# Windowed-attention scores in eight 64x32 tiles of 160 keys each, and a new instruction order

## Chip, core and metric

The kernel is one program on one core of a Trainium2 chip. The metric is device time in microseconds (us), from the first to the last instruction of a run, as the median of several runs. One execution was also profiled; all rows below come from that one.

## The reference, cut to what matters

Eight batches, eight heads, 576 positions, head width 64. The first half is causal attention with a window of 128 keys and a linear bias; its output `x` feeds four experts, each a full causal attention of width 64, mixed by the two best gates.

```python
# first half, per batch and head (window = 128)
scores = scale * np.matmul(q, k.transpose(0, 1, 3, 2))
mask = (rel >= 0) & (rel < window)              # rel = query position - key position
scores = np.where(mask, scores + bias[None], -1000000000.0)
attn = softmax(scores); attn_out = np.matmul(attn, v)
# second half, per expert e, x is (8, 576, 512)
q, k, v = x @ wq[e], x @ wk[e], x @ wv[e]
a = softmax(causal(scale * (q @ k.transpose(0, 2, 1))))
ye = a @ v @ wo[e]                               # added to out with the gate's weight where e is chosen
```

## The kernel before

**Work.** The first half goes by groups: one group is one batch and two heads, 32 groups in all. A group's queries stand in four blocks of 128 and a tail of 64. For block `i` the window reaches over the block's own 128 keys and the 128 before them, so `scores` (line 717) multiplies 128 queries by 256 keys (128 for block 0), once for each of the two heads. The operands are `e` (groups 0 to 3) or `r` (groups 4 to 31): one head lies in partitions 0 to 63, the other in 64 to 127, so each product is a 64x128 tile of TensorE (64 rows, 128 columns of weights), and the two heads use its two halves. The tail is one 128x128 product from `r` and `q`. The score blocks land in PSUM banks. `wrap` copies with a mask, so that of the 256 columns the 128 that row `r` needs stand in one place: row `r` of a block needs keys `r+1` to `r+128` of the 256. VectorE then adds the bias and takes the extremum (`softmax_block`), ScalarE does the exponential (`exp_block`), `normalise` multiplies by the reciprocal sum (`scl`: on GpSimd or ScalarE). TensorE transposes the result (`idt,p`), ScalarE, VectorE and GpSimd bring it to SBUF (`pa`), TensorE multiplies it by the values (`pa,vt`, two 128x64 tiles) and `xh` and its remainder `xl` are kept.

**The second half** projects `x` (`qkproj`, `vproj`: `WH`, `WL` with `xh`), forms the experts' scores (`moe_s`: `KSm,QSm`, 64x128 tiles; the tail `KSm,QBm`), normalises, transposes through DRAM (`d`, `mpt`) or on TensorE, multiplies by the values (`mpt,v`, 128x64 tiles) and by `wo` (`moe_wo`). Float32 products are recorded as two matmuls each; those in `float32r` as one.

**Order.** All engine work is first recorded as a list. Then `plan` builds a graph of it, gives each node a rank, and `schedule` walks through time with cost figures of its own, picks the node of highest rank on each engine, the PSUM bank of each result, and the engine of those operations that have alternatives (`nc.any`: a copy from PSUM on ScalarE or VectorE, a rescaling on GpSimd or ScalarE). On TensorE it groups the nodes by the shape of the tile (`_kind`) with a price for a change of it (`_enter`). Where TensorE has nothing to do early on, it adds a filling product on zeros (`fill`, `bank<-QBm` with 256 columns). The numbers in `K` steer all of this. All instructions leave through line 1465 (1478 in the changed file), so groups are told apart by tile names.

Of the kernel before, what the change touches and what calls it, by code (L numbers as in the profile page):

```python
# [34 lines left out]
K = {'dr': 385, 'S': 2, 'T': 2, 'A': 2, 'X': 1, 'M': 1, 'apv': 0, 'alag': 2, 'pvlag': 2, 'vorder': 0, 'na': 0, 'pp': 2, 'tp': 4, 'mp': 3, 'ta0': 0.08, 'ta1': 0.91, 'sa0': 0.1, 'sa1': 1.0, 'sb0': 0.68, 'sb1': 0.77, 'tb0': -0.03, 'tb1': 1.08, 'wo0': 0.1, 'wo1': 0.45, 'wa0': 0.05, 'wa1': 1.3, 'aa0': 0.0, 'aa1': 1.04, 'ab0': -0.04, 'ab1': 1.0, 'xp': 6, 'ts': 1, 'lead': 0, 'pa': 2, 'na0': 2, 'wb0': 0.18, 'wb1': 1.0, 'sh': 0, 'man': 1, 'mode': 'rank', 'wv': 1, 'off': {'AHTmsb': -51319, 'AHTmsc': 226585, 'AHTmsd': 57984, 'AHmsb': 962863, 'AHmsc': -1174046, 'AHmsd': 176548, 'ALTmvb': -352873, 'ALTmvc': 681549, 'ALTmvd': -720993, 'ALmvb': -58580, 'ALmvc': -343133, 'ALmvd': 387548, 'Ggb': -294268, 'Ggc': 358200, 'Ggd': 796547, 'Gvb': 50164, 'Gvc': 356650, 'Gvd': -900704, 'KSmsb': -134466, 'KSmsc': 71203, 'KSmsd': -949465, 'KSmvb': 878611, 'KSmvc': 564812, 'KSmvd': 177012, 'MPLgb': -196142, 'MPLgc': -640724, 'MPLgd': 354521, 'MPLsb': -745879, 'MPLsc': -467463, 'MPLsd': 612374, 'MPLvb': -896678, 'MPLvc': 231527, 'MPLvd': -176829, 'QBmgb': -157372, 'QBmgc': 543347, 'QBmgd': 601313, 'QBmvb': 23180, 'QSmsb': -53771, 'QSmsc': 238376, 'QSmsd': -140325, 'QSmvb': -403396, 'QSmvc': -572336, 'QSmvd': -1126436, 'Qvb': -1083103, 'Qvc': 419856, 'Qvd': 85696, 'WHga0': 215851, 'WHga1': -1349520, 'WHga2': -20302, 'WHga3': -216938, 'WLva0': -987256, 'WLva1': 222553, 'WLva2': -36747, 'WLva3': -289734, 'WOHgb': -356530, 'WOLvb': -286267, 'Wvb': 1153321, 'Wvc': -170954, 'Wvd': -272595, 'bdtgb': -10523, 'cntvb': -146833, 'cntvc': 20870, 'cntvd': 237025, 'dsb': 1203, 'dsc': -165933, 'dsd': 31497, 'dvsb': -495176, 'dvsc': 457438, 'esb': 163420, 'exgb': -68299, 'exgc': 22524, 'exgd': 302310, 'exsb': 101341, 'exsc': -235122, 'exsd': 567186, 'idtsb': 590241, 'lgvb': -151767, 'lgvc': 386501, 'lgvd': 265472, 'maltb': -8751, 'maltc': 334704, 'maltd': -97900, 'matb': -365698, 'matc': 248620, 'matd': -22341, 'mktsb': -419636, 'mpgb': -406012, 'mpgc': 613629, 'mpgd': -154987, 'mpsb': 945412, 'mpsc': 4558, 'mpsd': -362700, 'mptsb': -182897, 'mptsc': 801091, 'mptsd': 314174, 'mpvb': -134103, 'mpvc': 336130, 'mpvd': -599159, 'mrvb': -1116242, 'mrvc': -99062, 'mrvd': -1036577, 'msltb': -129432, 'msltc': -366459, 'msltd': 175381, 'msmvb': 369133, 'mstb': 1203485, 'mstc': 692927, 'mstd': 840517, 'mttd': -325265, 'mttsb': 168397, 'mxvb': -299213, 'mxvc': -478280, 'mxvd': 99527, 'otc': -605153, 'otd': -1396659, 'otsc': 150370, 'otsd': 92453, 'outsc': -133228, 'outsd': -181459, 'paga0': -503470, 'paga1': 249445, 'paga2': -267635, 'paga3': -222708, 'pagb': 181139, 'pagc': 147868, 'pasa0': -38196, 'pasa1': 37112, 'pasa2': -870775, 'pasa3': 155051, 'pasb': 555862, 'pasc': 26055, 'pava0': -620338, 'pava1': -187059, 'pava2': 773026, 'pava3': -655362, 'pavb': 704014, 'pavc': 122636, 'pga0': -2221003, 'pga1': -795897, 'pga2': -130731, 'pga3': -1738506, 'pgb': -53777, 'pgc': 76239, 'psa0': 28304, 'psa1': -185091, 'psa2': 204361, 'psa3': 128899, 'psb': -1536389, 'psc': -386534, 'pva0': 339625, 'pva1': -498595, 'pva2': 68261, 'pva3': 728830, 'pvb': -369118, 'pvc': -142760, 'qktb': -187519, 'qktc': -911093, 'qktd': -1759864, 'qsb': -417280, 'qsc': 71999, 'rsb': -258694, 'rsc': -219196, 'rva0': 51622, 'rva1': 381144, 'rva2': 332157, 'rva3': -218686, 'rvb': -1056049, 'rvc': 484891, 'smvb': 135492, 'sta0': 180586, 'sta1': 91875, 'sta2': 76259, 'sta3': 764898, 'stb': 1475626, 'stc': 351117, 'sva0': 248048, 'sva1': -621166, 'sva2': -209110, 'sva3': -150684, 'svb': -266514, 'svc': -1900487, 'tbtsb': -338384, 'tmsb': 211161, 'tmsc': 447992, 'tmsd': 570421, 'tmtsb': -328856, 'tta0': 166591, 'tta1': -745498, 'tta2': 206031, 'tta3': 487372, 'ttb': -169960, 'ttc': 1223111, 'vgd': 77695, 'vsb': 348165, 'vsc': 629445, 'vsd': 510506, 'vsgb': -166647, 'vsgc': 98885, 'vssb': -74263, 'vssc': 694024, 'vsvb': 85697, 'vsvc': 252966, 'vtb': 316160, 'vtc': 54818, 'vtd': 81004, 'vtsb': -411318, 'vtsc': -108070, 'vvd': -29753, 'wgb': -488048, 'wgc': 850675, 'wgd': -21990, 'wstsb': -513062, 'wsvb': 221204, 'wsvc': -637005, 'wsvd': -102434, 'xhsa0': 522390, 'xhsa1': -221939, 'xhsa2': -523460, 'xhsa3': 183211, 'xhsb': 570069, 'xhsc': 1038764, 'xhva0': 61127, 'xhva1': -6055, 'xhva2': 279616, 'xhva3': 568354, 'xhvb': 161674, 'xhvc': -251466, 'xta0': -614582, 'xta1': 56907, 'xta2': 434532, 'xta3': 445032, 'xtb': 217229, 'xtc': 297371, 'xtta0': -177787, 'xtta1': 546283, 'xtta2': 235747, 'xtta3': 245812}, 'cw': 12, 'lm': 15, 'f0': 900, 'f1': 69640, 'f2': 8574.9424, 'setup': 1254186.7966, 'wt': 0.7926, 'bv': -1660.3072, 'ba': -24824.2265, 'bp': -44128.4556, 'chn': 150, 'l0': 0.5, 'l1': 0.75, 'w0': 0.04, 'w1': 0.83, 'w2': 0.15, 'w3': 1.15, 'hs': 9.253065176954073e+41, 'bz': [21712, 2035, 1615], 'vl': 1, 'wd': 0, 'dx': 300, 'se': 0, 'gl': 1, 'rb': 3, 'early': 4, 'vb': 3, 'la': 4, 'fx': 1, 'fm': 1, 'pt': 7, 'q': 8888, 'ex': 0, 'rq': 0, 'o0': 1, 'dh': 1.6, 'eq': 1, 'wb': 1, 'tbf': 2, 'db': 4, 'es': 0, 'aft': 0, 'nl': 1, 'px': [7], 'ps': 1, 'pn': (), 'af': 210, 'an': 0.84, 'vs': 2, 'tc': 1.04, 'rl': 1.4, 'ku': 3, 'nat': 0, 'at': 32, 'ae': 32, 'xw': 1, 'sv': 1, 'as': 1, 'hold': 0.0, 'gw': 2.9095}  # L35
# [29 lines left out]
def _cost(e, m, a, k):  # L65
# [3 lines left out]
    if e == "tensor":  # L69
        if m == "transpose":  # L70
            return 108.5
        full = a[1].ap[0][1] == P
        wide = _free(a[1]) == P
        if a[1].dtype == F32R:
            return max(n * 0.4475 + 3, 109) if full else max(n * 0.4475 + 4, 110) / 2
        if not wide:
            return n / 1.2 + 3
        return (2 if full else 1) * (max(n / 1.2, 107) + 3)
# [18 lines left out]
def _kind(e, m, a):  # L97
    if e != "tensor":
        return 0
    if m == "transpose":  # L100
        return 1
    if a[1].ap[0][1] != P:
        return 2
    return 3 if _free(a[1]) != P else 1


def _enter(e, m, a):
    if e != "tensor":
        return 0
    return (ENTER, 200, 150)[_kind(e, m, a) - 1] if m != "transpose" else 155  # L110
# [97 lines left out]
def graph(ops, alt):  # L208
# [112 lines left out]
def schedule(g, rank, succ, setup=0.0, wt=0.5, bias=((0, 0, 0, 0, 0),) * 2, fill=(900, 60000, 9999), cw=6, hs=0):  # L321
# [46 lines left out]
    while done < n:  # L368
        while ev and ev[0][0] <= now:
            i = heapq.heappop(ev)[1]  # L370
            q = alts[i]
            if len(q) > 1:
# [9 lines left out]
                eng[i], cost[i], lock[i] = best[1], best[2], port[i][best[3]]  # L382
# [6 lines left out]
        for e in range(5):  # L389
            if not ready[e] or t[e] > now:  # L390
                continue
            if e == 0:
# [9 lines left out]
                sums = [0.0] * 4  # L402
# [99 lines left out]
def plan(ops, alt):  # L502
# [8 lines left out]
    for x in order:  # L511
# [39 lines left out]
def attn_moe_kernel(ctx, tc, hd, rd, vd, wall, wo, mk, tb, tm, mt, ident, out):  # L551
# [163 lines left out]
    def scores(g, u, s, n0):  # L715
# [4 lines left out]
        for i in (2 * u, 2 * u + 1):  # L720
# [324 lines left out]
    def moe_s(b, pr, blocks):  # L1045
# [507 lines left out]
```

## Time and profile before

| | us |
|---|---|
| median of three runs (lowest to highest) | 495.44 (494.18 to 495.81) |
| span of the profiled execution | 493.3 |
| TensorE matmuls busy | 480.1 |
| weight loads busy | 408.1 |
| VectorE busy | 366.6 |
| ScalarE busy | 331.1 |
| GpSimd busy | 259.5 |

The profiled execution's own time is its span, 493.3 us, from its first to its last instruction; the median of the runs is 2.1 us above it. Busy times of different engines overlap. A matmul's record reaches from its start to a modelled end behind the pipeline, so records of one engine overlap too: what a matmul costs is read from the distance of the starts.

### The profile page before, as it was taken

Reading aid. Unit: us, or ns where it says so; the run is one execution under the profiler, and the core shown is the slowest. Engines: PE = TensorE matmul, PEld = TensorE weight load, DVE = VectorE, ACT = ScalarE, POOL = GpSimd, SP = SyncE. Lnnn points to the kernel's source line nnn. Section 1 sums busy time; section 2 is a strip of 40 time slices with the busy share of each in tenths; the row PEclk is TensorE's granted clock in tenths of the full one; section 3 lists DMA queues with packets and bytes.
Section 4 is the critical chain, followed back from the end, with each engine's and each line's share of the span. In section 5 each row is a group of like instructions: output and inputs, shape, how many; then the busy total and the mean of one; then the engine's idle time right before and its main releaser. Section 6 shows DMA issues by size and latency. Waiting matters only on the chain.

```text
span 493.3 us, 13248 instructions
## 1 busy us (share of the span) xinstructions
PE 480.1 (97%) x4259; PEld 408.1 (83%) x4259; DVE 366.6 (74%) x1818; ACT 331.1 (67%) x1240; POOL 259.5 (53%) x572
## 2 busy tenths in 40 slices
PE   7889999999999999999999999999999999999995
PEld 6768988998797989888888888879879878898864
DVE  4577788889979798885959788797687868736510
ACT  3796578778758577773947758496685746536862
POOL 0796574657837529382573728375164836412340
PEclk9999999999999999999999999999999999999999
DMA  7868352575587976596938856688717463567023
GB/s 218 266 181 251 115 147 60 197 251 188 179 284 227 332 247 222 183 295 241 305 127 257 296 201 186 217 280 267 257 69 241 184 236 126 192 225 231 1 86 106
DMA packets 50853, 100.79 MB, mean 204 GB/s; under 512 B 4960, under 2 KB 28640, under 8 KB 50784
## 3 DMA queue, kind: packets, MB, share of 16 engines
q1 hardware_dynamic: 50704, 99.81, 61.8%
q8 instruction: 34, 0.56, 0.5%
q14 instruction: 35, 0.29, 0.2%
q10 hardware_dynamic: 80, 0.13, 0.1%
HBM read 62.05 MB, written 37.88 MB: 203 GB/s over the span
## 4 chain that ended last, share of the span: by engine, by line
PE 72%; DMA 10%; DVE 7%; ACT 6%; POOL 3%; SPq 1%; issue 1%; POOLq 0%; ACTq 0%; DVEq 0%
PE bank L1465 72%; DMA out<-ot 4%; DMA d<-W 2%; DMA e<-in_hd 2%; ACT p L1465 2%; ACT mp L1465 2%; DVE mp L1465 1%; DVE W L1465 1%; POOL p L1465 1%; DMA wst<-in_wall 1%; DVE p L1465 1%; ACT ot L1465 1%; SPq L1465 1%; DVE bank L1465 1%; DVE xh L1465 1%
## 5 line engine op out<-in xcount | busy, mean ns | idle before, releaser
L1465 ACT ACTIVATE p<-p,nm 128x128 f32<-128x128 f32 x288 | 113.1, 396 | 46.9 <-DVE nm L1465 44.9
L1465 POOL TENSOR_SCALAR p<-p,r 128x128 f32<-128x128 f32 x279 | 98.3, 374 | 50.8 <-ACT p L1465 16.5
L1465 POOL TENSOR_SCALAR mp<-mp,mr,w 128x384 f32<-128x384 f32 (+3 forms) x128 | 75.8, 608 | 50.3 <-DVE nm L1465 23.8
L1465 PE MATMUL bank<-xh,WH 128*128 128x288 f32 x512 | 90.0, 302 | 0.0
L1465 PEld LDWEIGHTS bank<-xh,WH 128*128 128x128 f32 x512 | 75.1, 189 | 2.3 <-issue 1.4
L1465 ACT ACTIVATE mp<-mp,mnm 128x512 f32<-128x512 f32 (+3 forms) x128 | 70.2, 551 | 9.5 <-DVE mnm L1465 9.4
L1465 DVE CUSTOM_DVE_ANT_0 p<-bank,tbt 128x128 f32<-128x128 f32 x288 | 70.2, 280 | 0.7
L1465 PE MATMUL bank<-pa,vt 128*64 128x256 f32 (+2 forms) x768 | 59.6, 311 | 1.9 <-DVE pa L1465 1.6
L1465 DVE STREAM_TRANSPOSE W<-mp 128x128 f32<-128x128 f32 (+1 forms) x112 | 53.7, 494 | 8.3 <-DMA d<-W 5.1
L1465 PEld LDWEIGHTS bank<-pa,vt 128*64 128x64 f32 x768 | 43.3, 137 | 18.6 <-DVE pa L1465 2.5
L1465 PE MATMUL bank<-WH,xh 128*128 128x260 f32 x288 | 58.2, 293 | 0.3 <-ACT ot L1465 0.3
L1465 DVE COPY_PREDICATED bank<-mkt,bank 128x256 f32<-128x256 int32 (+2 forms) x160 | 47.7, 325 | 11.7 <-PE bank L1465 11.5
L1465 DVE CUSTOM_DVE_ANT_0 mp<-bank,mtt 128x512 f32<-128x512 f32 (+3 forms) x128 | 54.7, 485 | 1.2 <-PE bank L1465 1.1
L1465 ACT ACTIVATION_READ_ACCUMULATOR p<-p,nm 128x1 f32 x288 | 55.1, 191 | 0.0
L1465 POOL TENSOR_SCALAR_AFFINE_SELECT pa<-pa 128x512 f32<-128x512 f32 x64 | 39.7, 635 | 23.8 <-ACT pa L1465 22.1
L1465 PE MATMUL bank<-xh,WL 128*128 128x288 f32 x256 | 51.7, 297 | 0.0
L1465 PE MATMUL bank<-mpt,v 128*64 128x64 f32 (+4 forms) x576 | 49.3, 319 | 0.2
L1465 PE MATMUL bank<-r 64*128 64x256 f32 (+1 forms) x448 | 49.1, 358 | 0.0
L1465 PE MATMUL bank<-idt,p 128*128 128x128 f32 x288 | 47.2, 277 | 1.6 <-POOL p L1465 1.5
L1465 PEld LDWEIGHTS bank<-WH,xh 128*128 128x128 f32 x288 | 44.8, 189 | 2.2 <-DVE mnm L1465 0.9
L1465 PEld LDWEIGHTS bank<-mpt,v 128*64 128x64 f32 x576 | 27.4, 137 | 21.4 <-issue 15.3
L1465 PEld LDWEIGHTS bank<-r 64*128 64x128 f32 x448 | 37.0, 187 | 5.9 <-issue 2.0
(98 smaller groups left out, 918.7 us busy)
## 6 DMA issues: line engine op xcount, KB each, us to landing
d<-W SPq DMA_DIRECT2D x28, 832.0 KB, 4.7
mpt<-d SPq DMA_DIRECT2D x28, 832.0 KB, 5.4
vt<-in_vd SPq DMA_DIRECT2D x32, 320.0 KB, 3.8
out<-ot SPq DMA_DIRECT2D x32, 256.0 KB, 2.9
r<-in_rd SPq DMA_DIRECT2D x28, 288.0 KB, 4.0
r<-in_hd SPq DMA_DIRECT2D x56, 128.0 KB, 3.9
dv<-vs SPq DMA_DIRECT2D x35, 128.0 KB, 2.8
v<-dv SPq DMA_DIRECT2D x7, 640.0 KB, 4.6
```

The costliest lines, as they stand in the source:

```text
L1465: getattr(getattr(tc.nc, e), m)(*a, **k)
```

## The change

Each 128-query block is cut in four quarters of 32 queries. Quarter `x` (its first query) needs only keys `x+1` to `x+159` of the 256, so it gets its own product of 32 queries by 160 keys (block 0: all 128 keys), written to its own 32 PSUM partitions. With two heads that makes eight products of 64x32 tiles where there were two of 64x128. The rest of the 256 columns is not written any more, so each PSUM bank is written once at the beginning with zeros (`blank`, eight products of 512 columns). `moe_s` gets the same loop, but `K["ms"]` is 1, so it does what it did. `_kind` gives 64x32 tiles a kind of their own.

`K` has new values: besides the ranks by category that were there (`off`), a number for each node (`nd`) that is added to its rank, and for some nodes the alternative to use (`nf`). So the order of every engine is another, and so is the engine of a number of operations.

```diff
-K = {'dr': 385, 'S': 2, 'T': 2, 'A': 2,
...
+K = {'nd': {0: 2095482, 1: 230515, 2: 147409, 3: 778716,
...
+'qs': 4, 'ms': 1, 'dr': 385, 'S': 2, 'T': 2, 'A': 2,
...
 def _kind
     if a[1].ap[0][1] != P:
-        return 2
+        return 4 if _free(a[1]) != P else 2
...
 def schedule
-                eng[i], cost[i], lock[i] = best[1], best[2], port[i][best[3]]
+                x = K["nf"].get(i, best[3])
+                eng[i], cost[i], lock[i] = *q[x], port[i][x]
...
 def schedule_k
+    rank = [r + K["nd"].get(i, 0) for i, r in enumerate(rank)]
...
 def plan
+        if i == alt["blank"][0]:
+            out += [_place(alt["blank"][1], lambda v: alt["banks"][k]) for k in range(BANKS)]
...
 def warm
+        nc.alt["blank"] = (first["QB"], ("tensor", "matmul", (z, QB[:, 0, 0, :], QB.rearrange("p a b n -> p (a b n)")), dict(start=True, stop=True)))
...
 def scores
-            for h in range(2):
-                d = r[D * h : D * h + D]
-                nc.tensor.matmul(ss[h][:, o : o + n], d[:, P * (i + h) : P * (i + h + 1)], d[:, k0 : k0 + n], start=True, stop=True)
+            w = P // K["qs"]
+            for x in range(0, P, w):
+                for h in range(2):
+                    d = r[D * h : D * h + D]
+                    q0, m = P * (i + h) + x, n - P + w if i else n
+                    nc.tensor.matmul(ss[h][x : x + w, o + x * (n > P) : o + x * (n > P) + m], d[:, q0 : q0 + w], d[:, k0 + x * (n > P) : k0 + x * (n > P) + m], start=True, stop=True)
...
 def zero
+        first["QB"] = len(nc.ops)
         nc.vector.memset(QB.bitcast(F32), 0.0)
```

The order on TensorE at the start of the program, before: filling products, then the scores of group 0 (`e0`).

```order
L1465 MATMUL bank0_83<-QBm_106 128x256 x15
L1465 MATMUL bank0_83<-e0_115 128x256
L1465 MATMUL bank1_84<-e0_115 128x256
...
L1465 MATMUL bank2_85<-e0_115 128x128
L1465 MATMUL bank3_86<-e0_115 128x128
...
L1465 MATMUL bank4_87<-e1_118 128x256
```

The same place in the changed kernel; a size is output partitions x columns.

```order
L1478 MATMUL bank0_83<-QBm_106 128x512
...
L1478 MATMUL bank7_90<-QBm_106 128x512
L1478 MATMUL bank0_83<-QBm_106 128x256 x15
L1478 MATMUL bank0_83<-e0_115 32x128
L1478 MATMUL bank1_84<-e0_115 32x128
...
L1478 MATMUL bank0_83<-e0_115 32x160
L1478 MATMUL bank1_84<-e0_115 32x160
```

Eight products of 512 columns now stand ahead of the fifteen fillings, and the first block stands as eight products of 128 columns (two of the eight are shown).

Later on TensorE, before: the transposes of groups 6 and 7 (`p6`, `p7`) between the value projections, and the scores of group 8 (`r8`) with the first expert scores behind them.

```order
L1465 MATMUL bank1_84<-idt_91,p6_184 128x128 x4
L1465 MATMUL bank6_89<-idt_91,p6_184 128x128 x4
...
L1465 MATMUL bank4_87<-idt_91,p7_193 128x128 x4
L1465 MATMUL bank6_89<-idt_91,p7_193 128x128 x4
...
L1465 MATMUL bank3_86<-r8_172,q8_173 128x192
L1465 MATMUL bank5_88<-r8_172 128x256
L1465 MATMUL bank6_89<-r8_172 128x256
...
L1465 MATMUL bank0_83<-KSm_108,QSm_105 128x512
```

The same groups in the changed kernel.

```order
L1478 MATMUL bank6_89<-idt_91,p7_193 128x128
L1478 MATMUL bank0_83<-xh3_168,WL_98 128x288
...
L1478 MATMUL bank4_87<-xh0_144,WH_97 128x288
L1478 MATMUL bank6_89<-idt_91,p7_193 128x128 x2
L1478 MATMUL bank7_90<-idt_91,p7_193 128x128
...
L1478 MATMUL bank3_86<-idt_91,p6_184 128x128
L1478 MATMUL bank5_88<-r8_172,q8_173 128x192
...
L1478 MATMUL bank7_90<-r8_172 32x128
L1478 MATMUL bank6_89<-r8_172 32x128
...
L1478 MATMUL bank0_83<-xh0_144,WL_98 128x288
```

The transposes that stood in fours are cut into ones and twos with projections between them, and the scores of group 8 stand alone between 128x128 products, where before the expert scores followed in the same tile shape.

## Rows read from the trace of the kernel before

**Rows 1.** the page: busy time of each engine, and the chain by engine
```profile
PE 480.1 (97%) x4259; PEld 408.1 (83%) x4259; DVE 366.6 (74%) x1818; ACT 331.1 (67%) x1240; POOL 259.5 (53%) x572
...
PE 72%; DMA 10%; DVE 7%; ACT 6%; POOL 3%; SPq 1%; issue 1%; POOLq 0%; ACTq 0%; DVEq 0%
```

**Rows 2.** stretches: length, busy of PE, PEld, DVE, ACT, POOL, clock, DMA
```profile
24.00:30.00 6.00, 5.66 (x49) 3.69 (x45) 4.91 (x34) 6.00 (x27) 6.00 (x5) 1.00 0.62 176
...
100.00:200.00 100.00, 99.58 (x912) 85.71 (x911) 87.06 (x435) 71.90 (x282) 63.83 (x143) 1.00 0.73 244
```

**Rows 3.** TensorE group by shape: tile, result, count, busy, mean ns
```profile
L1465 PE MATMUL bank<-r 64*128 64x256 f32 x336 | 47.0, 386 | 0.0
```

**Rows 4.** timeline of TensorE (start, length, count): half groups, one pair of scores
```profile
55.94 1.14 PE L1465 MATMUL bank<-r 64*128 64x256 f32 x8
57.01 0.41 PE L1465 MATMUL bank<-xh,WH 128*128 128x288 f32 x1
...
62.62 0.93 PE L1465 MATMUL bank<-r 64*128 64x128 f32 x8
63.48 0.44 PE L1465 MATMUL bank<-pa,vt 128*64 128x256 f32 x2
...
108.88 0.38 PE L1465 MATMUL bank<-r 64*128 64x256 f32 x2
```

**Rows 5.** timeline of TensorE: score groups, alone and joined to expert scores
```profile
108.56 1.79 PE L1465 MATMUL bank<-r 64*128 64x256 f32 x16
110.28 0.44 PE L1465 MATMUL bank<-pa,vt 128*64 128x256 f32 x2
...
70.97 1.79 PE L1465 MATMUL bank<-r 64*128 64x256 f32 x16
72.41 1.05 PE L1465 MATMUL bank<-KSm,QSm 64*128 64x512 f32 x6
```

**Rows 6.** weight loads by shape
```profile
L1465 PEld LDWEIGHTS bank<-r 64*128 64x128 f32 x448 | 37.0, 187 | 5.9 <-issue 2.0 <-DVE nm L1465 0.3 <-DVE mr L1465 0.3
...
L1465 PEld LDWEIGHTS bank<-mpt,v 128*64 128x64 f32 x576 | 27.4, 137 | 21.4 <-issue 15.3 <-DVE mnm L1465 1.4 <-DVE mr L1465 0.5
```

**Rows 7.** timeline of TensorE: twenty short products in two 128x64 tiles
```profile
304.76 0.80 PE L1465 MATMUL bank<-mpt,v 128*64 128x64 f32 x20
305.39 0.39 PE L1465 MATMUL bank<-pa,vt 128*64 128x256 f32 x2
```

**Rows 8.** timeline of TensorE: single transposes between projections
```profile
102.45 0.30 PE L1465 MATMUL bank<-xh,WH 128*128 128x288 f32 x1
102.58 0.27 PE L1465 MATMUL bank<-idt,p 128*128 128x128 f32 x1
...
102.83 0.29 PE L1465 MATMUL bank<-xh,WL 128*128 128x288 f32 x1
...
158.34 0.37 PE L1465 MATMUL bank<-WL,xh 128*128 128x260 f32 x1
158.54 0.27 PE L1465 MATMUL bank<-idt,p 128*128 128x128 f32 x1
...
158.77 0.55 PE L1465 MATMUL bank<-KSm,QBm 128*128 128x288 f32 x3
```

**Rows 9.** timeline of TensorE at the start
```profile
1.68 3.42 PE L1465 MATMUL bank<-QBm 128*128 128x256 f32 x15 [1.68 <-DVE QBm L1465]
5.63 1.79 PE L1465 MATMUL bank<-e 64*128 64x256 f32 x16 [0.53 <-DMA e<-in_hd]
8.70 0.48 PE L1465 MATMUL bank<-e 64*128 64x256 f32 x1 [1.28 <-DMA e<-in_hd]
```

**Rows 10.** ScalarE, VectorE and GpSimd groups by shape
```profile
L1465 ACT ACTIVATE p<-p,r 128x128 f32<-128x128 f32 x9 | 3.3, 405 | 0.0
...
L1465 DVE TENSOR_TENSOR xh<-bank,xh 128x512 fp32r<-128x512 f32 x32 | 21.7, 680 | 13.2 <-ACT xh L1465 13.0
...
L1465 POOL TENSOR_SCALAR p<-p,r 128x128 f32<-128x128 f32 x279 | 98.3, 374 | 50.8 <-ACT p L1465 16.5 <-DVE r L1465 11.7 <-PE bank L1465 11.1
```

More of the change, by code (lines that the diff above doesn't have):

```diff
@@ L32 @@
 EPS = 1e-9
-K = {'dr': 385, 'S': 2, 'T': 2, 'A': 2, 'X': 1, 'M': 1, 'apv': 0, 'alag': 2, 'pvlag': 2, 'vorder': 0, 'na': 0, 'pp': 2, 'tp': 4, 'mp': 3, 'ta0': 0.08, 'ta1': 0.91, 'sa0': 0.1, 'sa1': 1.0, 'sb0': 0.68, 'sb1': 0.77, 'tb0': -0.03, 'tb1': 1.08, 'wo0': 0.1, 'wo1': 0.45, 'wa0': 0.05, 'wa1': 1.3, 'aa0': 0.0, 'aa1': 1.04, 'ab0': -0.04, 'ab1': 1.0, 'xp': 6, 'ts': 1, 'lead': 0, 'pa': 2, 'na0': 2, 'wb0': 0.18, 'wb1': 1.0, 'sh': 0, 'man': 1, 'mode': 'rank', 'wv': 1, 'off': {'AHTmsb': -51319, 'AHTmsc': 226585, 'AHTmsd': 57984, 'AHmsb': 962863, 'AHmsc': -1174046, 'AHmsd': 176548, 'ALTmvb': -352873, 'ALTmvc': 681549, 'ALTmvd': -720993, 'ALmvb': -58580, 'ALmvc': -343133, 'ALmvd': 387548, 'Ggb': -294268, 'Ggc': 358200, 'Ggd': 796547, 'Gvb': 50164, 'Gvc': 356650, 'Gvd': -900704, 'KSmsb': -134466, 'KSmsc': 71203, 'KSmsd': -949465, 'KSmvb': 878611, 'KSmvc': 564812, 'KSmvd': 177012, 'MPLgb': -196142, 'MPLgc': -640724, 'MPLgd': 354521, 'MPLsb': -745879, 'MPLsc': -467463, 'MPLsd': 612374, 'MPLvb': -896678, 'MPLvc': 231527, 'MPLvd': -176829, 'QBmgb': -157372, 'QBmgc': 543347, 'QBmgd': 601313, 'QBmvb': 23180, 'QSmsb': -53771, 'QSmsc': 238376, 'QSmsd': -140325, 'QSmvb': -403396, 'QSmvc': -572336, 'QSmvd': -1126436, 'Qvb': -1083103, 'Qvc': 419856, 'Qvd': 85696, 'WHga0': 215851, 'WHga1': -1349520, 'WHga2': -20302, 'WHga3': -216938, 'WLva0': -987256, 'WLva1': 222553, 'WLva2': -36747, 'WLva3': -289734, 'WOHgb': -356530, 'WOLvb': -286267, 'Wvb': 1153321, 'Wvc': -170954, 'Wvd': -272595, 'bdtgb': -10523, 'cntvb': -146833, 'cntvc': 20870, 'cntvd': 237025, 'dsb': 1203, 'dsc': -165933, 'dsd': 31497, 'dvsb': -495176, 'dvsc': 457438, 'esb': 163420, 'exgb': -68299, 'exgc': 22524, 'exgd': 302310, 'exsb': 101341, 'exsc': -235122, 'exsd': 567186, 'idtsb': 590241, 'lgvb': -151767, 'lgvc': 386501, 'lgvd': 265472, 'maltb': -8751, 'maltc': 334704, 'maltd': -97900, 'matb': -365698, 'matc': 248620, 'matd': -22341, 'mktsb': -419636, 'mpgb': -406012, 'mpgc': 613629, 'mpgd': -154987, 'mpsb': 945412, 'mpsc': 4558, 'mpsd': -362700, 'mptsb': -182897, 'mptsc': 801091, 'mptsd': 314174, 'mpvb': -134103, 'mpvc': 336130, 'mpvd': -599159, 'mrvb': -1116242, 'mrvc': -99062, 'mrvd': -1036577, 'msltb': -129432, 'msltc': -366459, 'msltd': 175381, 'msmvb': 369133, 'mstb': 1203485, 'mstc': 692927, 'mstd': 840517, 'mttd': -325265, 'mttsb': 168397, 'mxvb': -299213, 'mxvc': -478280, 'mxvd': 99527, 'otc': -605153, 'otd': -1396659, 'otsc': 150370, 'otsd': 92453, 'outsc': -133228, 'outsd': -181459, 'paga0': -503470, 'paga1': 249445, 'paga2': -267635, 'paga3': -222708, 'pagb': 181139, 'pagc': 147868, 'pasa0': -38196, 'pasa1': 37112, 'pasa2': -870775, 'pasa3': 155051, 'pasb': 555862, 'pasc': 26055, 'pava0': -620338, 'pava1': -187059, 'pava2': 773026, 'pava3': -655362, 'pavb': 704014, 'pavc': 122636, 'pga0': -2221003, 'pga1': -795897, 'pga2': -130731, 'pga3': -1738506, 'pgb': -53777, 'pgc': 76239, 'psa0': 28304, 'psa1': -185091, 'psa2': 204361, 'psa3': 128899, 'psb': -1536389, 'psc': -386534, 'pva0': 339625, 'pva1': -498595, 'pva2': 68261, 'pva3': 728830, 'pvb': -369118, 'pvc': -142760, 'qktb': -187519, 'qktc': -911093, 'qktd': -1759864, 'qsb': -417280, 'qsc': 71999, 'rsb': -258694, 'rsc': -219196, 'rva0': 51622, 'rva1': 381144, 'rva2': 332157, 'rva3': -218686, 'rvb': -1056049, 'rvc': 484891, 'smvb': 135492, 'sta0': 180586, 'sta1': 91875, 'sta2': 76259, 'sta3': 764898, 'stb': 1475626, 'stc': 351117, 'sva0': 248048, 'sva1': -621166, 'sva2': -209110, 'sva3': -150684, 'svb': -266514, 'svc': -1900487, 'tbtsb': -338384, 'tmsb': 211161, 'tmsc': 447992, 'tmsd': 570421, 'tmtsb': -328856, 'tta0': 166591, 'tta1': -745498, 'tta2': 206031, 'tta3': 487372, 'ttb': -169960, 'ttc': 1223111, 'vgd': 77695, 'vsb': 348165, 'vsc': 629445, 'vsd': 510506, 'vsgb': -166647, 'vsgc': 98885, 'vssb': -74263, 'vssc': 694024, 'vsvb': 85697, 'vsvc': 252966, 'vtb': 316160, 'vtc': 54818, 'vtd': 81004, 'vtsb': -411318, 'vtsc': -108070, 'vvd': -29753, 'wgb': -488048, 'wgc': 850675, 'wgd': -21990, 'wstsb': -513062, 'wsvb': 221204, 'wsvc': -637005, 'wsvd': -102434, 'xhsa0': 522390, 'xhsa1': -221939, 'xhsa2': -523460, 'xhsa3': 183211, 'xhsb': 570069, 'xhsc': 1038764, 'xhva0': 61127, 'xhva1': -6055, 'xhva2': 279616, 'xhva3': 568354, 'xhvb': 161674, 'xhvc': -251466, 'xta0': -614582, 'xta1': 56907, 'xta2': 434532, 'xta3': 445032, 'xtb': 217229, 'xtc': 297371, 'xtta0': -177787, 'xtta1': 546283, 'xtta2': 235747, 'xtta3': 245812}, 'cw': 12, 'lm': 15, 'f0': 900, 'f1': 69640, 'f2': 8574.9424, 'setup': 1254186.7966, 'wt': 0.7926, 'bv': -1660.3072, 'ba': -24824.2265, 'bp': -44128.4556, 'chn': 150, 'l0': 0.5, 'l1': 0.75, 'w0': 0.04, 'w1': 0.83, 'w2': 0.15, 'w3': 1.15, 'hs': 9.253065176954073e+41, 'bz': [21712, 2035, 1615], 'vl': 1, 'wd': 0, 'dx': 300, 'se': 0, 'gl': 1, 'rb': 3, 'early': 4, 'vb': 3, 'la': 4, 'fx': 1, 'fm': 1, 'pt': 7, 'q': 8888, 'ex': 0, 'rq': 0, 'o0': 1, 'dh': 1.6, 'eq': 1, 'wb': 1, 'tbf': 2, 'db': 4, 'es': 0, 'aft': 0, 'nl': 1, 'px': [7], 'ps': 1, 'pn': (), 'af': 210, 'an': 0.84, 'vs': 2, 'tc': 1.04, 'rl': 1.4, 'ku': 3, 'nat': 0, 'at': 32, 'ae': 32, 'xw': 1, 'sv': 1, 'as': 1, 'hold': 0.0, 'gw': 2.9095}
@@ L74, in _cost @@
         if a[1].dtype == F32R:
-            return max(n * 0.4475 + 3, 109) if full else max(n * 0.4475 + 4, 110) / 2
+            return max(n * 0.4475 + 3, 109) if full else max(n * 0.4475 + 4, 110) / 2 * _free(a[1]) / P
+        if not full and not wide:
+            return n / 1.2 * _free(a[1]) / P + 6
         if not wide:
@@ L109, in _enter @@
         return 0
-    return (ENTER, 200, 150)[_kind(e, m, a) - 1] if m != "transpose" else 155
+    return (ENTER, 200, 150, 200)[_kind(e, m, a) - 1] if m != "transpose" else 155
 def _half(a):
@@ L253, in graph @@
             if e == "tensor":
-                f += _free(a[0]) * (2 if m == "transpose" else 1 if a[1].dtype == F32R else 4) * a[1].ap[0][1] / P
+                f += _free(a[0]) * (2 if m == "transpose" else 1 if a[1].dtype == F32R else 4) * a[1].ap[0][1] / P * (_free(a[1]) / P if a[1].ap[0][1] != P else 1)
         cols.append(f)
@@ L401, in schedule @@
                     continue
-                sums = [0.0] * 4
+                sums = [0.0] * 5
                 for q in c:
@@ L1060, in moe_s @@
             for k, (x, y) in enumerate(TERMS):
-                for j in range(2):
-                    d = slice(D * j, D * j + D)
-                    nc.tensor.matmul(
-                        ss[j][:, o : o + n], QS[d, pr, x, P * i : P * (i + 1)], KS[d, pr, y, :n], start=(k == 0), stop=(k == 2)
-                    )
+                w = P // K["ms"]
+                for z in range(0, P, w):
+                    for j in range(2):
+                        d = slice(D * j, D * j + D)
+                        nc.tensor.matmul(
+                            ss[j][z : z + w, o : o + n], QS[d, pr, x, P * i + z : P * i + z + w], KS[d, pr, y, :n], start=(k == 0), stop=(k == 2)
+                        )
             jobs.append((i, n, o))
```

1 line of the change is left out of this document (added).

## The prediction, written before the changed kernel ran

> **What bounds the kernel now.** First the page: TensorE's matmuls are busy for 480.1 of 493.3 us, and the chain that ended last runs over PE for 72% [rows 1]. Then the stretches: from 100 to 200 us matmuls fill 99.58 of 100 us at clock 1.00, the 2.4 GHz level, while VectorE has 13% left and ScalarE and GpSimd more; only early, as at 24 to 30 us, do other engines fill up [rows 2]. So from about 35 us to the last products a TensorE nanosecond saved or added is one of the result, as long as results arrive in time. Because records overlap, I then took the timeline and measured distances of starts.
>
> **What a score group costs now.** A group makes 16 records (336 of the 256-column kind in 28 groups [rows 3], that is 12, and four of 128). The two heads' records start together: one lasts 386 ns on average [rows 3], and the two from 108.88 span 0.38 us together [rows 4]. So a group is eight slots, two heads in each. Two half groups give the slots' size: four of 256 columns go from 55.94 to the next start at 57.01, 1.07 us; two of 128 and two of 256 go from 62.62 to 63.48, 0.86 us [rows 4]. The difference, 0.21 us, is 2 x 128 columns, 0.82 to 0.84 ns a column: 0.107 us for a slot of 128 and 0.214 for one of 256, plus some 2 ns. The sum is 6 x 0.215 + 2 x 0.109 = 1.51 us. The whole group takes 1.72 us from its start to the next one (108.56 to 110.28) [rows 5]: 0.21 us is the price of going into this tile shape and out of it. Joined to the expert scores, which have the same shape, it takes 1.44 (70.97 to 72.41) [rows 5] and pays no exit.
>
> **Term 1, the products.** Eight 64x32 products of 160 columns replace two of 256. If all eight tiles stream at once, a slot takes 160 x 0.834 = 133 ns, a block two slots, and block 0 (still 128 columns) 2 x 107. How eight tiles go side by side no row shows. From below: no loss, 6 x 133 + 2 x 107 = 1.01 us, 0.50 less than now. From above: the densest row I have, twenty short records in 0.63 us (304.76 to 305.39), 31.5 ns a record [rows 7]; the 64 new records at that pace take 2.02 us, 0.51 more than now. That row is itself bound by its streams (64 columns x 0.834 = 53 ns for two), so it is a loose end. Nearer is the row of the pair: two records that start within 10 ns, with only some 2 ns lost per slot of two [rows 4]. I give each record of a slot 1.2 ns, so 143 and 117 ns, 6 x 143 + 2 x 117 = 1.09 us, and 7 x 6 ns once until the last tile is done: 1.14 us. Saved 0.377 us a group, for 32 groups **-12.1 us** (ends -16 and +16).
>
> One thing speaks against it. In the Trainium skill, "TensorE: Matmul & The Clock Gate", section "Wait — 56ns, not 53.3ns?", says that starts come no closer than about 25 ns however short a matmul is; part 3 of that page, on packing, gives about 4 ns between tiles. By the second the sum stays near mine; by the first, 64 x 25 ns = 1.60 us a group would be an estimate of +2.9 us for this term. The pair of [rows 4] contradicts the first between two tiles, but no row here contradicts it as a mean over many records.
>
> **Term 2, changes of tile shape.** Counted over the two orders, TensorE changes shape 105 times before and 129 after, since scores no longer share a shape with the expert scores. 24 x 0.21 us [rows 5] = +5.0. Against it, a run of scores begins with weights of 32 columns, not 128: 187 against 137 ns for 128 and 64 columns [rows 6] is 0.8 ns a column, so 75 ns less in each of 33 runs, -2.5. Together **+2.5 us** (ends 0 and +5).
>
> **Term 3, transposes in small pieces.** Runs of transposes away from filling products grow from 76 to 109. One can be free: projection to projection over one transpose, 102.45 to 102.83, is 0.38 us, just 0.13 + 0.11 + 0.13. Or, when they alternate, 158.34 to 158.77 is 0.43 against 0.12 + 0.11 + 0.12 [rows 8]. 33 pieces at 0 to 0.09, I take 0.06: **+2.0 us** (ends 0 and +3).
>
> **Term 4, start and end.** The 15 fillings of 256 columns take 3.42 us, 0.2 us each, then PE waits 0.53 us for the first data, and 1.28 us for the second group's at 8.70 [rows 9]. Eight zeroing products of 512 columns at twice that add about 3.3 us; less the 0.53 the first scores come up to 2.8 us later, and less if the products behind run at the 0.12 us that 256 columns take elsewhere (0.834 ns a column, halved for `float32r`). The delay lies beside the loads of the second group, and shorter scores give 0.4 us back; late next would be VectorE's first blocks. I take 0.3 us. Planned fillings go from 89 to 92, 3 x 0.12 = 0.4. At the end the experts' tail product stands directly before the six last products, so its copy and subtraction are exposed once, some 0.5 us (ends 0 and 1). Together **+1.2 us** (ends 0 and +3.5).
>
> **Other engines, costed at nothing.** The order shows 77 more rescalings on ScalarE at 405 ns and 77 fewer on GpSimd at 374 [rows 10], and 56 copies on VectorE that ScalarE made before. Priced by elements after the 512-column row of 680 ns [rows 10], those are about +27 us on VectorE (367 to 394), +6 on ScalarE, -28 on GpSimd. What hides them is their slack: VectorE's 87% in 100 to 200 us [rows 2] becomes (87 + 5.4) / 98.5, some 94%. If this cover fails, it is the third rival. DMA issues are as many as before, 309.
>
> **Sum.** -12.1 + 2.5 + 2.0 + 1.2 = -6.4 us. The span goes from 493.3 to 486.9, and with the 2.1 us between span and median the time from 495.44 to **489.0 us**, 1.3% faster. What a measurement can tell from no change is 0.3%, 1.5 us.
>
> **Rivals.**
>
> *Tiles quite without loss, small costs hidden.* Term 1 is -16, terms 2 to 4 half, -13 in all: 482 us. For it: the pair of [rows 4] loses next to nothing. Against: the new edges are there in the order.
>
> *Dispatch bounds the packed scores: slower.* TensorE must take 64 matmuls and 64 weight loads a group instead of 16 and 16. If a record costs more than a fixed time, the eight tiles queue behind it. The point that decides: the other terms cost 5.7 us, 0.18 a group, so a group must stay under 1.51 - 0.18 = 1.33 us, 21 ns a record. At 25 to 31.5 ns a record term 1 is +3 to +16, and the time 504 to 517 us. For it: no row here sustains less than 31.5 ns a record [rows 7]. Against: that row was bound by its streams, and pairs start within 10 ns [rows 4].
>
> *VectorE becomes late.* At 94% in the busiest stretch, each result that waits holds a PSUM bank, and TensorE behind it. If a quarter of the added 27 us is seen, +6.5: 495.5 us, no change. For it: the chain already passes VectorE for 7% [rows 1]. Against: TensorE stood still for 0.4 us in 100 [rows 2] under 87%.
>
> *The tiles don't overlap at all but for the two heads.* Then four quarters of two slots each, 3 x 8 x 133 + 8 x 107 = 4.0 us a group, +2.5 x 32 = +80: about 580 us. Against: the heads' tiles overlap now [rows 4].
>
> **How the numbers follow.** Forecast (484 to 493.9) 0.58; without loss (below 484) 0.12; VectorE late, or gain eaten by edges (494 to 497), 0.10; dispatch 0.16; no overlap 0.04. Faster by over 0.3%: 0.58 + 0.12 + 0.02 of the third = 0.72; same 0.08; slower 0.16 + 0.04 = 0.20. The range goes from 481 (0.02 below) to 497, and leaves out the 0.2 above.
>
> **What would show it.** Term 1: records of 64x32 tiles, a group alone in 1.1 to 1.4 us from its first start to the next shape's, and starts within a slot some 6 ns apart. If dispatch binds, starts of the 64 records lie evenly 20 to 30 ns apart. Term 2: 0.1 to 0.2 us around each run. Term 3: gaps beside single transposes. Term 4: first scores after 6.5 us. VectorE late: waits of TensorE's loads for VectorE over some microseconds, now under one in 100. What would make me wrong most is the pace of dispatch; next, idle TensorE in the first 45 us, where the new order may gain or lose what I didn't count.

## The result, and the profile after

The changed kernel takes 487.55 us (median of four runs, 486.81 to 490.28) against 494.81 us (four runs, 493.85 to 495.81): a ratio of 0.987, 95% interval 0.985 to 0.990. It is faster by 1.3%, and 489.0 us was predicted. Its profiled span is 486.1 us, against 493.3 before.

The page of the changed kernel: busy time of each engine, then the chain by engine.

```profile
span 486.1 us, 16340 instructions
...
PE 473.4 (97%) x5806; PEld 401.6 (83%) x5806; DVE 389.4 (80%) x1874; ACT 333.5 (69%) x1260; POOL 234.7 (48%) x496
...
PE 74%; DMA 11%; DVE 9%; ACT 3%; SPq 1%; issue 1%; ACTq 0%
```

TensorE gives out 1547 more matmuls than in [rows 1] and is busy 6.7 us less. VectorE takes 23 us more and GpSimd 25 less (27 and 28 were forecast from the order). The same two stretches as in [rows 2], after:

```profile
24.00:30.00 6.00, 5.36 (x94) 2.83 (x92) 5.63 (x42) 5.64 (x27) 6.00 (x7) 1.00 0.67 196
100.00:200.00 100.00, 99.74 (x1329) 84.01 (x1328) 91.97 (x451) 77.52 (x302) 48.12 (x104) 1.00 0.74 242
```

VectorE stands at 92% in the long stretch (94 was forecast) and TensorE at 99.7, so VectorE isn't late there.

A score group that stands alone, in the timeline of TensorE of the changed kernel (start, length, count; whole records only). The first two rows are the group and its successor. The others are the same row in windows that end earlier: the next two in windows that end at 131.62 and 131.66 us, the last two in windows at 131.84 and at 131.90 us. Each counts what has started by then.

```profile
131.61 1.26 PE L1478 MATMUL bank<-r 64*32 64x128 f32 x64
132.80 0.44 PE L1478 MATMUL bank<-pa,vt 128*64 128x256 f32 x2
...
131.61 0.30 PE L1478 MATMUL bank<-r 64*32 64x128 f32 x2
...
131.61 0.34 PE L1478 MATMUL bank<-r 64*32 64x128 f32 x8
...
131.61 0.45 PE L1478 MATMUL bank<-r 64*32 64x128 f32 x16
...
131.61 0.59 PE L1478 MATMUL bank<-r 64*32 64x128 f32 x24
```

The whole group takes 1.19 us from its first start to the next shape's, where [rows 5] have 1.72. Eight records, one for each tile, start within 0.05 us; then nothing starts until the slot has streamed. The third slot of eight, the first with 160 columns, moves the last end by 0.14 us. So the eight tiles stream at once: by the starts of the trace's records, a slot of 160 columns takes 136 ns and one of 128 takes 108, against 133 and 107 by the columns alone. Only the ends of the run differ: its first slot is some 25 ns longer, and from the start of its last slot to the next shape it is 272 ns, 136 more than a slot; together that is 0.16 us. Within a slot the records start 6 to 7 ns apart.

The weight loads of those groups, and the products by shape, in the changed kernel:

```profile
L1478 PEld LDWEIGHTS bank<-r 64*32 64x32 f32 x1792 | 27.0, 106 | 6.5 <-issue 2.6 <-ACT ot L1478 1.1 <-DVE pa L1478 0.4
...
L1478 PE MATMUL bank<-r 64*32 64x160 f32 x1344 | 31.7, 299 | 0.0
```

A load of 32 columns takes 106 ns, in line with 187 and 137 for 128 and 64 [rows 6].

**Where the 7.15 us of span came from.** Records overlap, so I took for each matmul the distance from its start to the next one's, and added these up by what the matmul does. The table splits each kernel at its first projection; e2 is an experiment told below, with the changed order and the old products. All are us, worked out from the starts in the traces.

| | before | after | e2 |
|---|---|---|---|
| all up to the first projection | 44.71 | 45.43 | 45.74 |
| behind it: scores | 42.22 | 33.57 | 46.17 |
| projections | 165.56 | 167.07 | 166.86 |
| transposes | 31.33 | 29.62 | 28.20 |
| experts' scores with tails | 49.09 | 50.30 | 49.86 |
| the other products | 154.60 | 155.04 | 154.97 |
| from the last start to the end | 5.78 | 5.11 | 5.11 |
| span | 493.29 | 486.14 | 496.91 |

The gain is in the scores of the 26 groups behind the first projection. The 6 groups ahead of it fall as well, from 13.91 to 8.60 us (waits for loads included), but the first projection doesn't come earlier: it starts 0.72 us later than before.

Each column is one execution, and its waits differ from the next one's. How much shows in two experiments told below. e3 gives every engine the same list as the changed kernel but for fifteen products at the start; behind the first projection its scores cost 32.14 us instead of 33.57, its experts' scores 51.67 instead of 50.30, and all classes together 1.7 us more. e6 has the same list up to the first projection, and starts it at 44.54 us instead of 45.43. So of the rows above only the scores, and the last one (5.11 or 5.12 us in every execution with the new order, 5.76 to 5.78 in the old), stand clear of this; the differences of 0.5 to 1.7 us in the other rows don't.

### The profile page after: what moved, and what is told of

Its sections match the earlier page's. It is cut to its first block, busy times and chain, and to the rows that moved or that the text cites. A ratio compares the mean times of both kernels' runs of the same rounds, so it can differ in the third digit from the quotient of the medians.

```text
span 486.1 us, 16340 instructions
## 1 busy us (share of the span) xinstructions
PE 473.4 (97%) x5806; PEld 401.6 (83%) x5806; DVE 389.4 (80%) x1874; ACT 333.5 (69%) x1260; POOL 234.7 (48%) x496
## 4 chain that ended last, share of the span: by engine, by line
PE 74%; DMA 11%; DVE 9%; ACT 3%; SPq 1%; issue 1%; ACTq 0%
PE bank L1478 74%; DMA out<-ot 4%; DMA d<-W 3%; DVE W L1478 2%; ACT p L1478 2%; SPq L1478 1%; DMA wst<-in_wall 1%; DVE mp L1478 1%; DMA e<-in_rd 1%; DMA r<-in_rd 1%; DVE p L1478 1%; DVE bank L1478 1%; DMA e<-in_hd 1%; DVE xh L1478 1%; DVE pa L1478 1%
## 5 line engine op out<-in xcount | busy, mean ns | idle before, releaser
L1478 POOL TENSOR_SCALAR p<-p,r 128x128 f32<-128x128 f32 x202 | 71.6, 372 | 92.8 <-DVE r L1478 51.4
L1478 PE MATMUL bank<-xh,WH 128*128 128x288 f32 x512 | 110.8, 303 | 0.0
L1478 POOL TENSOR_SCALAR mp<-mp,mr,w 128x512 f32<-128x512 f32 (+3 forms) x128 | 75.9, 608 | 45.6 <-DVE mr L1478 35.7
L1478 PEld LDWEIGHTS bank<-xh,WH 128*128 128x128 f32 x512 | 83.2, 189 | 2.4 <-issue 1.3
L1478 PE MATMUL bank<-xh,WL 128*128 128x288 f32 x256 | 73.7, 302 | 0.0
L1478 PE MATMUL bank<-WH,xh 128*128 128x260 f32 x288 | 61.8, 292 | 0.1
L1478 DVE COPY_PREDICATED bank<-mkt,bank 128x128 f32<-128x128 int32 (+2 forms) x160 | 48.7, 326 | 12.9 <-PE bank L1478 12.7
L1478 PE MATMUL bank<-idt,p 128*128 128x128 f32 x288 | 52.3, 278 | 2.9 <-POOL p L1478 1.6
L1478 PEld LDWEIGHTS bank<-xh,WL 128*128 128x128 f32 x256 | 47.3, 189 | 0.8 <-issue 0.3
L1478 PE MATMUL bank<-WL,xh 128*128 128x260 f32 x160 | 43.4, 288 | 0.0
```

Source lines behind the costliest of these rows:

```text
L1478: getattr(getattr(tc.nc, e), m)(*a, **k)
```

## The experiments

All were timed in five rounds beside the kernel before (median 494.99 us beside e1 to e4, 495.67 beside the others); the ratios are to it. The edits of e1 to e4, e6 and e9 act on the ordered list of instructions.

**e1: the new products in the old order.** Every old pair of score products is cut where it stood; the eight zeroing products are added behind the first `memset`.

```diff
+    def cut(pair, w):
+        wide = _free(pair[0][2][0]) > P
+        m = P + w if wide else P
+        for x in range(0, P, w):
+            for e, _, (o, l, r), k in pair:
+                c = x if wide else 0
+                yield e, "matmul", (part(o, w, x, m, c), part(l, D, 0, w, x), part(r, D, 0, m, c)), k
...
+            if len(held) == 2:
+                out_ += cut(held, 32)
```

> The instruction order of the kernel before, with each block's pair of 64x128 products replaced where it stands by eight 64x32 products, and the eight zeroing products at the start. Theory A (the products give the gain; after the first 45 us, in which nothing is won, 26 groups save 0.50 us each in streams, -13, and about 16 new edges to the expert scores cost 0.2 us each, +3): 484 to 487 us, no worse than the changed kernel. Rival B (the gain is the new order's, and cut products without it are eaten by new edges and by VectorE): 492 us or more.

Measured: 491.22 us, ratio 0.993 (0.991 to 0.995), between the two forecasts. Behind the first projection the scores fall by 8.8 us, but the other classes rise by 6.8: projections 2.3, experts' scores with tails 2.3, transposes 0.8, experts' values 1.2. The chain of e1 by engine:

```profile
PE 62%; DVE 14%; DMA 10%; ACT 8%; POOL 3%; issue 1%; SPq 1%; POOLq 0%; ACTq 0%; DVEq 0%
```

The chain passes TensorE for 62% where it was 72 [rows 1], and VectorE for 14% where it was 7: it fits that in an order made for longer scores TensorE comes to results that aren't there yet. The longest of its waits by releaser:

```profile
PE bank L1493 <- POOL p L1493: 2.5, 6, 1.1
PE bank L1493 <- DVE QBm L1493: 1.7, 1, 1.7
PE bank L1493 <- DVE xh L1493: 1.0, 2, 0.7
PE bank L1493 <- DMA mpt<-d: 0.9, 2, 0.6
```

In the changed kernel the waits for `p` on GpSimd come to 1.6 us, for `xh` and `mpt` to none. Visible waits are 1.1 us more than before, not 6.8. Both kernels have the same order, so the other products can be compared one by one: 1.0 of the 6.8 us lies at the ten places where experts' scores run into scores, which are now a change of shape. Most of the rest lies in some two dozen products that come 0.1 to 0.5 us later. The modelled ends of the records cover the shorter of these gaps, so what each of them waited for is not shown.

**e2: the old products in the new order.** Four quarters are merged again into one product of 128 queries by 256 keys.

```diff
+    W_ = 128
...
+        if m == "matmul" and a[0].ap[0][1] == 32:
+            x = a[0].offset // 512
+            if x % W_:
+                continue
+            n = P + W_ if _free(a[0]) > P else P
+            a = (part(a[0], W_, n), part(a[1], D, W_), part(a[2], D, n))
```

> The instruction order of the changed kernel, with each block's eight products joined again to two of 64x128 with all 256 columns. Theory A: each of 26 groups takes 0.50 us more for its streams and 0.07 for its longer weight load at the start, +13 to +15 on the changed kernel, so 500 to 502 us, slower than the kernel before. Rival B (the order gives the gain): 487 to 491 us.

Measured: 497.64 us, ratio 1.007 (1.004 to 1.009), 2.4 us under the forecast. By itself the new order is a loss. The table above shows where: scores +3.95 us. Two parts make it up. Behind the first projection TensorE goes through 44 stretches of this tile shape instead of 32, and 12 more at the 0.21 us of [rows 5] are 2.5 us. And two runs of scores hold a wait for `ot` of ScalarE, by the starts 1.4 us in all, where no run of scores of the kernel before holds one (timeline of TensorE of e2):

```profile
274.88 0.50 PE L1492 MATMUL bank<-WOH,AHm 128*128 128x512 f32 x1 [0.88 <-ACT ot L1492]
...
343.67 0.93 PE L1492 MATMUL bank<-r 64*128 64x128 f32 x8 [0.36 <-ACT ot L1492]
```

From e2 to the changed kernel nothing but the products differs, and the scores behind the first projection fall by 12.6 us, 0.485 a group.

**e4: four tiles of 64x64, 192 keys each.** As e2, with the width 64: half the records, each slot 32 columns longer.

```diff
-    W_ = 128
+    W_ = 64
```

> The changed kernel's order with 64x64 tiles: four products of 64 queries by 192 keys a block, half as many matmuls and weight loads. If columns streamed set the time of a block, a slot takes 160 ns instead of 133, 0.16 us more a group, and 26 groups outside the start give +4.2 us: 491 to 492.5. If the number of records sets it, half the records make it faster or the same: 487.5 or less.

**e9: eight tiles, but all 256 columns.** The number of records of the change, the columns of before.

```diff
+        if m == "matmul" and a[0].ap[0][1] == 32 and _free(a[0]) > P:
+            x = a[0].offset // 512
+            a = (part(a[0], x, 2 * P), a[1], part(a[2], x, 2 * P))
```

> The changed kernel's order with eight 64x32 products a block, each over all 256 columns instead of its 160. Streams bound: a slot takes 213 ns again, 0.48 us more a group; 26 groups outside the start give +12.5, less what waits there were, so 497 to 500 us, and the scores outside the start take 46 us, as with two products a block, though there are four times as many records. Records bound: each record would add to that, and the scores would take clearly more than 46 us.

The group alone from the result, in e2, then e4, then e9, each with its successor (timeline of TensorE):

```profile
135.04 1.79 PE L1492 MATMUL bank<-r 64*128 64x128 f32 x16
136.76 0.44 PE L1492 MATMUL bank<-pa,vt 128*64 128x256 f32 x2
```

```profile
131.34 1.42 PE L1492 MATMUL bank<-r 64*64 64x128 f32 x32
132.69 0.44 PE L1492 MATMUL bank<-pa,vt 128*64 128x256 f32 x2
```

```profile
134.25 1.74 PE L1488 MATMUL bank<-r 64*32 64x128 f32 x64
135.93 0.65 PE L1488 MATMUL bank<-pa,vt 128*64 128x256 f32 x4
```

Measured: e4 489.66 us, ratio 0.989 (0.987 to 0.991); e9 496.97 us, 1.005 (1.002 to 1.007). In e4 the group takes 1.35 us, 0.16 more than with eight tiles: 6 slots by 32 columns by 0.834 ns is 0.16. Half the records buy nothing. Its time rose by only 2.1 us where 26 such groups were to give 4.2, below the forecast, and its interval overlaps that of the changed kernel; where the other half went is not shown, as the execution profiled was the longest of e4 (492.0 us) and holds a wait of 2.30 us for `ot`. In e9 the 64 records take 1.68 us, less than the 16 of e2 (1.72). The columns of a slot decide, and the number of records doesn't. Behind the first projection the scores cost 46.17 us in e2 and 44.22 in e9, 1.95 less. Part of that is in the loads: the first slot of a lone group takes 134 ns in e9 and 214 in e2, which fits a load that is shorter by 81 ns (106 against 187); its last slot takes 40 ns more. That leaves 0.045 us a run, 1.2 in all; the rest is mostly e2's longer waits for `ot`. From e9 to the changed kernel, where only columns go, it is 10.65 us.

**e3: without the fifteen first fillings.** It leaves out products on zeros whose result nobody reads.

```diff
+        if not seen and o[1] == "matmul" and _free(o[2][0]) == 2 * P:
+            continue
```

> The changed kernel without the fifteen filling products that stand before the first scores (they compute nothing that is used). If the zeroing products delay the whole start, the first scores come at 5.6 us instead of 7.3 and the time falls by 1.2 to 1.7 us. If the loads and ScalarE set the first 45 us, the first scores come as early and the time stays within 0.5 us.

Measured: 489.15 us, ratio 0.987 (0.984 to 0.990), not to be told from the changed kernel; the interval is too wide to settle a gain of 1.2 us by itself. The start of the changed kernel in the timeline, then that of e3:

```profile
1.65 5.76 PE L1478 MATMUL bank<-QBm 128*128 128x512 f32 x23 [1.65 <-DVE QBm L1478]
7.34 1.29 PE L1478 MATMUL bank<-e 64*32 64x128 f32 x64
8.56 0.59 PE L1478 MATMUL bank<-e,q 128*128 128x192 f32 x2
9.58 0.59 PE L1478 MATMUL bank<-e,q 128*128 128x192 f32 x2 [0.43 <-DMA q<-in_hd]
```

```profile
1.66 3.78 PE L1485 MATMUL bank<-QBm 128*128 128x512 f32 x8 [1.66 <-DVE QBm L1485]
5.37 1.78 PE L1485 MATMUL bank<-e 64*32 64x128 f32 x64
7.08 0.59 PE L1485 MATMUL bank<-e,q 128*128 128x192 f32 x2
9.46 0.66 PE L1485 MATMUL bank<-e,q 128*128 128x192 f32 x2 [1.78 <-DMA q<-in_hd]
```

The first scores come 1.97 us earlier, and the second group's tail 0.12 us: the same load of `q` ends both. The delay that the zeroing brings is hidden by the loads. But e3 differs in one more thing: behind the wait of 1.78 us the granted clock of e3 stood at its lower level, 1.2 GHz, from 9.85 to 13.26 us, and the second group's scores took 2.2 us instead of 1.2. The changed kernel shows no such stretch there.

**e6: the transposes put together.** Transposes into one bank are moved to the last of them wherever no other engine reads the bank in between; runs of transposes away from fillings fall from 109 to 78.

```diff
+        if turn_(o) and len(open_[b]) > 1:
+            q = open_[b]
...
+                move[n] = move.pop(q[-2], []) + [q[-2]]
+                drop.add(q[-2])
```

> The changed kernel's order, with the transposes of one PSUM bank moved to the place of their last one, after the first projection only; runs of transposes fall from 109 to 78. Theory (a piece cut off costs 0.06 us of TensorE): 31 runs less give -1.9 us, about 485.7. Rival (the pieces stood where TensorE would have waited, or the later results hold up ScalarE and VectorE): the same or up to 3 us more.

Measured: 490.02 us, ratio 0.990 (0.988 to 0.992). The gain of 1.9 us that a cost of 0.06 us a piece would give is not there; whether e6 is slower than the changed kernel is not clear, as the intervals overlap. The projections do get cheaper, by 1.25 us (165.82 us; the five executions with the uncut new order show 166.8 to 167.6). But the transposes themselves cost 1.5 us more, the experts' scores 1.8 and `wo` 2.2, of which this one wait of e6 is nearly all (timeline of TensorE, then the chain of e6 up to it):

```profile
378.07 0.40 PE L1503 MATMUL bank<-WOH,ALm 128*128 128x512 f32 x1
380.67 0.54 PE L1503 MATMUL bank<-xh,WH 128*128 128x288 f32 x2 [2.19 <-DVE ot L1503]
```

```profile
368.74 8.39 DMA d<-W
...
379.44 1.18 DVE ot L1503 x2
...
380.67 9.74 PE bank L1503 x124
```

VectorE, which copies `ot`, had waited for a transfer to `d` that took 8.39 us. The same transfer, issued 0.3 us later, took 4.40 us in the changed kernel, and 6.34 in e3. So this wait comes from a transfer whose length differs between executions, and no run shows that a moved transpose made a copy late. What e6 shows is that joining the pieces brought no gain.

**e5 and e8: the scheduler with its rules alone.** e5 has the old numbers of `K`, e8 the new ones; both have the new products and neither has the table by node.

```diff
-K = {'nd': {0: 2095482, 1: 230515, 2: 147409, 3: 778716,
...
+K = {'nd': {}, 'nf': {},
```

> The changed kernel's code with the scheduling numbers of the kernel before, and no number for single nodes; the schedule is made anew with these for the eight-tile products. If the new numbers only had to fit the cheaper scores and the scheduler does that by itself, 486 to 489 us, as the changed kernel. If the numbers node by node are worth what the old order lost with the new products (491.2 against 487.6), 490 to 493 us.

> The changed kernel with its new numbers by category, but without the two tables for single nodes. If the tables carry the order, 492 us or more, as the categories were fitted together with them; if the categories do, 488 to 491 us.

Measured: e5 503.10 us, ratio 1.017 (1.014 to 1.019); e8 515.14 us, 1.041 (1.037 to 1.044). Both are slower than the kernel before, e5 beyond both of its forecasts, although the score products in them are the cheap ones (40.9 and 43.1 us in all, 42.2 in the changed kernel, 56.1 before). In e5 this one wait is the longest, and in e8 TensorE stands still for 19.2 us in all, 6.4 in the changed kernel (timeline of e5; then two of the waits of e8):

```profile
474.13 0.40 PE L1478 MATMUL bank<-WOH,ALm 128*128 128x512 f32 x1
478.04 0.33 PE L1478 MATMUL bank<-idt,mp 128*128 128x128 f32 x1 [3.51 <-POOL mp L1478]
```

```profile
PE bank L1478 <- POOL p L1478: 4.9, 7, 1.4
PE bank L1478 <- DVE nm L1478: 4.8, 9, 1.0
```

Behind that wait, from 479.48 to 486.31, the granted clock of e5 stood at its lower level, 1.2 GHz, as well. So the table by node is part of the gain: with the same other numbers and without it the ratio is 1.041, with it 0.987.

## Why the prediction was right, point by point

The time, 487.55 us for 489.0, and the sum, -7.15 us of span for -6.4, came out, by the mechanism that was named: fewer columns a slot. That the sum is so near is in part luck, as errors in it cancel. The terms compare so, in us:

| term | forecast | measured | from |
|---|---|---|---|
| 1, the products | -12.1 | -10.65 | scores, e9 to after |
| 2, changes of shape, less the weight loads | +5.0 - 2.5 | +3.95 - 1.95, waits included | scores, before to e2, e2 to e9 |
| 3, transposes in pieces | +2.0 | +1.45 | all other classes behind the first projection |
| 4, start and end | +1.2 | +0.05 | +0.72 and -0.67 |

**Term 1.** The mechanism held: slots of eight tiles, bound by the columns of one. Two sizes were off and nearly cancel, which is luck. I gave each record 1.2 ns, so 143 and 117 ns a slot; they take 136 and 108, hardly more than the columns. A group of eight slots and no end would thus be 1.03 us, not 1.14, and the saving 0.48, not 0.377. And I counted 32 groups where 26 to 28 count. 26 times 0.48 is 12.5 us, and 10.65 were measured: two runs of scores of the changed kernel hold 1.2 us of waits for `ot` of ScalarE, which e9 doesn't show (timeline of TensorE).

```profile
266.46 0.50 PE L1478 MATMUL bank<-WOH,AHm 128*128 128x512 f32 x1 [0.45 <-ACT ot L1478]
...
334.48 0.72 PE L1478 MATMUL bank<-r 64*32 64x128 f32 x32 [0.78 <-ACT ot L1478]
```

The first four groups stand where TensorE isn't what the end waits for. The chain of the changed kernel there (start, length, what), and behind it the place in the chain of the kernel before where TensorE takes over:

```profile
12.05 5.92 DMA e<-in_rd
17.99 6.63 DMA wst<-in_wall
24.64 0.83 ACT WH L1478
25.48 2.21 ACT p L1478 x11
...
28.49 2.62 ACT p L1478 x12
31.10 0.47 ACT xh L1478
31.57 1.46 ACT p L1478 x7
...
33.86 2.52 PE bank L1478 x20
```

```profile
32.03 17.98 PE bank L1465 x171
```

It goes over loads until 24.6 us and over ScalarE until 33.9, where TensorE takes over, 1.8 us later than before. Two more groups stand behind that and ahead of the first projection, at 38.58 and 42.26 us; what they save makes up 1.1 of the 1.8. I had said myself that a TensorE nanosecond counts "from about 35 us", and still multiplied by all groups. And ScalarE, which I had put at nothing, has a longer part of the start: up to 50 us the chain passes its work on `p` for 14.3%, before for 3.9%.

**Dispatch** was the rival that I thought likeliest, and it is refuted: 64 records with their 64 loads take 1.19 us, 19 ns each, under the 21 from which it would have decided, and e4 and e9 show that even those 19 are the streams'. So the 31.5 ns a record of my densest row, [rows 7], were not a pace that records can't beat. The rule against the change, from the Trainium skill, "TensorE: Matmul & The Clock Gate", section "Wait — 56ns, not 53.3ns?", that starts come no closer than about 25 ns, does not hold between tiles in this trace: 6 to 7 ns apart within a slot, 19 as a mean. Part 3 of that page, with about 4 ns between tiles, is nearer.

**Term 2** was right in kind, and near in size by luck. The 0.21 us of [rows 5] is the price of going into a shape and out of it, two changes, and I multiplied it by all 24 changes. Behind the first projection there are 12 more stretches, 2.5 us instead of 5.0; that e2 still shows 3.95 is owed to its waits for `ot`. With the new products an edge costs less: a lone group's 1.19 us less 1.03 leaves 0.16. The loads seem to give 0.072 us a run over 27 runs, forecast 0.075, but a lone group shows only 0.04 (1.72 to 1.68), and the rest is waits.

**Term 3** is not confirmed, though its sum is near. The transposes, which I thought dearer, cost 1.7 us less; projections (+1.5) and experts' scores (+1.2) cost more, and all three are of the size by which executions differ. Of these, 1.25 us of the projections go away when the pieces are joined (e6), so 31 fewer runs are worth 0.04 us each there, but the kernel doesn't get faster. Whether the pieces as a whole cost anything stays open.

**Term 4** counted costs that are hidden. The first scores came at 7.34 us (forecast: after 6.5), and in e3's trace the second group hardly gains by an earlier start. The 0.72 us at the first projection is within what executions differ (e6 against the changed kernel, 0.89). The experts' tail product at the end did not lengthen it: from the last start to the end it is 5.11 us, 5.78 before.

**VectorE late** is refuted as a whole: TensorE's visible waits for VectorE, but for the first, are under 2 us in the changed kernel. **No loss at all** (482) was right about the tiles and wrong about the edges.

What stays open: what exactly sets the first 45 us. The rows show loads, then ScalarE, and the new products in the old order (e1) reach the first projection 2.05 us earlier than the changed kernel does, of which executions alone can make 0.9. An order that has both was not tried.

## What to carry to other kernels

In this kernel, products on parts of TensorE's array that stream together cost the columns of one of them: cut a product into tiles that each see only the columns they need, and count the stretches of a tile shape and the weight loads, not the records. Multiply a price by what it was measured on (a stretch, not a change), and a saving only by the places where that engine is what the end waits for. Before a class of products is said to cost 1 us more, look how far two executions of the same list differ. And when a step gets cheaper, the order made for the dearer one gives much of it back (e1 -0.7%, e2 +0.7%, both together -1.3%), so judge the two together.

## What the runs showed that I had not expected

Four times as many matmuls and weight loads of a quarter of the width cost nothing (e9 against e2: 1.68 against 1.72 us a group); I had priced them at 1.2 ns a record. And a weight load of a quarter of the columns is, as a record, more than half as long (106 ns for 32 columns, 187 for 128), yet eight of them, one for each tile, lie beside the streams: a slot with eight of them is only 3 ns longer than its columns (136 against 133).
